# A prefetch hint on each engine for the branch over the general path, in an attention and gated feed-forward kernel

## The chip, the cores and the metric

The kernel runs on one core of a Trainium2 chip. The metric is the device time of one execution in microseconds; several runs are taken and their median is given. One further execution is recorded by the hardware profiler. Its trace names the engines PE (TensorE matmul), PEld (TensorE weight load), DVE (VectorE), ACT (ScalarE), POOL (GpSimd) and SP (SyncE); a trailing q (SPq, PEldq) marks an engine's instruction queue, in which branches, semaphore waits and DMA issues show.

## What is computed

For each of four batches, 32 inducing points attend to 12416 tokens of width 128, and the tokens attend to the result. A gated feed-forward layer with 1536 hidden units follows.

```python
h = mab(I, x)                      # softmax(I x^T * scale) x
y = mab(x, h)                      # softmax(x h^T * scale) h
gate = np.maximum(y @ w_gate, 0.0)
val = y @ w_val
out = (gate * val) @ w_out         # 49664 x 128
```

## The kernel before, in words

There are two ways through the program. `quadratic_kernel` computes the whole output by a form that holds as long as the sign of the gate of every hidden unit is the same for all tokens of a batch; four tests, one per batch, collect in `fine` for how many hidden units that is shown. At its end `left` is the number of units for which it is not (L1496 to L1511). `general_kernel` computes everything again in the ordinary way and runs only where `left` is above zero:

```python
left = quadratic_kernel(tc, *args)
with tc.If(left > 0):
    general_kernel(tc, *args)
```

The number is loaded into a register of each engine (L1512), each engine compares and branches (L1735), and with the inputs of this case all of them jump over the general path. The code of both ways lies one behind the other in each engine's program, and behind it the end of the program (L1762). On the short side of the branch each engine waits on one or more semaphores and goes on to the end; SP, which issues the stores, waits there for the eight DMA lanes of its transfers, one EVENT_SEMAPHORE for each.

In the way that runs, the tokens of a batch come in 12 blocks. For each block four pairs of score matmuls (L1341) are taken through an exponential on ACT (L1350), and the outputs of 128 tokens are summed by two runs of small matmuls (L1398); the second run stands behind a wait for the first (`after`). Three such outputs on each side make a unit. A unit is finished by a reciprocal `r{b}.{u}` (L1425) and a division `d{b}.{u}` (L1430) on VectorE, 16 units in a batch, and is then stored by SP (L1454; for the last two units of all, in four smaller stores, L1442).

Nothing reorders this work afterwards: the kernel schedules by hand. Each step is an `op` with its engine, its inputs and a function that emits its instructions. `plan.order` merges five fixed sequences, one for each engine, into one order by estimated starting times, and the loop at L1514 emits the steps in it:

```python
for o in plan.order(BEGIN, SEQUENCES, NEAR):
    if o.warm:
        keep_busy(*o.warm)
    if o.emit:
        o.emit()
```

`d3.13` (`B` is 4) is the third last division. In that order the last instructions ahead of it are, on ACT, the last exponential of the kernel; on VectorE the reciprocal `r3.13`; on SP the second store of unit 11's pair; on POOL the last step of the last test; on TensorE the end of one run of eight output matmuls, directly ahead of another run of eight.

Of the kernel before, what the change touches and what calls it, by code (L numbers as in the profile page):

```python
# [295 lines left out]
def quadratic_kernel(tc, x, inducing, moe_w_gate, moe_w_val, moe_w_out, out):  # L296
    with ExitStack() as ctx:
        return quadratic_body(
            ctx, tc, x, inducing, moe_w_gate, moe_w_val, moe_w_out, out
        )  # L300


def quadratic_body(ctx, tc, x, inducing, moe_w_gate, moe_w_val, moe_w_out, out):
    nc = tc.nc
    B, N, C = x.shape
# [85 lines left out]
    def main(shape, dtype, name):  # L391
        return mp.tile(shape, dtype, name=name)
# [83 lines left out]
    SYNC = mybir.DependencyInfo(mybir.DependencyClass.Sync, mybir.DependencyReason.DATA)  # L476
# [19 lines left out]
    def keep_busy(n, bank, part):  # L496

        for _ in range(4 * n if part else n):
            if part:
                pe.matmul(AL[:, bank, 400:BLK], ones16, ones16[:, 0 : BLK - 400], start=True, stop=True)  # L500
            else:
                pe.matmul(
                    AL[:, bank, :], ones16, ones16.unsqueeze(1).broadcast_to([P, 4, P]),
                    start=True, stop=True,
                )
# [989 lines left out]
    left = main([P, 1], mybir.dt.int32, "left")  # L1495
# [16 lines left out]
    op("load", "SP", 0.1, lambda: conds.append(nc.values_load(left[0:1, 0:1])), [(a, 1.5)])  # L1512
    quadratic_body.plan = plan
    for o in plan.order(BEGIN, SEQUENCES, NEAR):  # L1514
        if o.warm:
            keep_busy(*o.warm)
        if o.emit:
            o.emit()
# [205 lines left out]
def kernel(  # L1724
    tc: tile.TileContext,
    x: bass.AP,
    inducing: bass.AP,
    moe_w_gate: bass.AP,
    moe_w_val: bass.AP,
    moe_w_out: bass.AP,  # L1730
    out: bass.AP,
):
    args = (x, inducing, moe_w_gate, moe_w_val, moe_w_out, out)
    left = quadratic_kernel(tc, *args)
    with tc.If(left > 0):  # L1735
        general_kernel(tc, *args)


# [28 lines left out]
```

## Time and profile before

| | us |
|---|---|
| three runs, median | 270.16 |
| three runs, lowest and highest | 267.34 and 270.39 |
| the profiled execution | 268.36 |
| its span, first to last instruction | 266.5 |

TensorE is busy for 241.9 us of the span (91%), ACT for 222.7 (84%), VectorE for 180.0 (68%), GpSimd for 84.5 (32%). These shares count neither branches nor semaphore waits nor the issue of DMAs, so a stretch at the end in which only such instructions run shows as idle on every engine. The chain of waits, followed back from the last computation, gives TensorE 69% of the span, DMA 10%, ACT 9% and VectorE 4%. DMA moves 49.78 MB; two of its queues carry instructions and not data, and are listed as q8 and q14.

### The profile page before, as it was taken

What the parts mean: (1) busy time and instruction counts of PE and PEld (TensorE: products, weight loads), DVE (VectorE), ACT (ScalarE), POOL (GpSimd) and SP (SyncE); (2) the same over time, 40 slices, a digit from 0 to 9 for tenths busy, and PEclk for the clock granted to TensorE, in tenths of its full rate; (3) what the DMA queues carried; (4) which work ended last, traced back from release to release, by engine and by line L of the source; (5) the groups of instructions that cost most, each with busy time, mean ns of one, the idle gap of its engine ahead of it and who ended that gap; (6) DMA issues with size and microseconds to landing.
All of it is one profiled execution on the core that took longest, in us unless ns stands there. A gap on an engine that the chain in (4) does not pass through costs nothing.

```text
span 266.5 us, 12469 instructions
## 1 busy us (share of the span) xinstructions
PE 241.9 (91%) x5668; PEld 182.7 (69%) x5668; DVE 180.0 (68%) x377; ACT 222.7 (84%) x265; POOL 84.5 (32%) x145
## 2 busy tenths in 40 slices
PE   6889797889699999999999979999999999999970
PEld 2676565558476778777568867677777768878850
DVE  4457597785437898845779858755789895565550
ACT  3664798767669999999999968999999999999920
POOL 4476120399013000596130000197020008912000
PEclk9999999999869999999999999999999999999996
DMA  7999999959996986349999994033514333363552
GB/s 252 422 344 158 213 215 210 202 101 147 194 290 148 275 149 243 85 129 220 196 217 278 308 206 174 15 121 123 233 61 191 126 121 123 121 247 122 199 219 75
DMA packets 42653, 49.78 MB, mean 187 GB/s; under 512 B 29121, under 2 KB 30305, under 8 KB 42593
## 3 DMA queue, kind: packets, MB, share of 16 engines
q1 hardware_dynamic: 37680, 38.18, 47.5%
q0 software_dynamic: 4864, 10.72, 23.8%
q8 instruction: 46, 0.75, 1.2%
q14 instruction: 15, 0.11, 0.1%
q10 hardware_dynamic: 48, 0.02, 0.0%
HBM read 27.80 MB, written 25.43 MB: 200 GB/s over the span
## 4 chain that ended last, share of the span: by engine, by line
PE 69%; DMA 10%; ACT 9%; DVE 4%; issue 3%; SPq 2%; POOL 0%; ACTq 0%; DVEq 0%
PE AL L1398 35%; PE AL L1341 14%; ACT F L1350 7%; DMA F<-in_x_dram 6%; PE AL L1137 3%; DMA xTr<-x16r 3%; PE AL L925 2%; PE AL L957 2%; DMA out_dram<-osb 2%; PE AL L825 2%; PE AL L794 2%; DVE osb L1430 1%; PE AL L1156 1%; PE AL L500 1%; DVE u L1070 1%
## 5 line engine op out<-in xcount | busy, mean ns | idle before, releaser
L1350 ACT ACTIVATE F<-AL 128x1024 f16<-128x1024 f32 x192 | 184.4, 1037 | 15.7 <-PE AL L1341 12.8
L1398 PE MATMUL AL<-T,F 64*128 64x129 f16 x3456 | 136.3, 220 | 4.7 <-issue 3.3
L1398 PEld LDWEIGHTS <-F 64*128 64x128 f16 x3456 | 109.0, 95 | 34.4 <-PE AL L1398 20.5
L1341 PE MATMUL AL<-S,pairs 64*128 64x512 f16 x384 | 74.9, 382 | 1.4 <-ACT F L1350 0.6
L1430 DVE TENSOR_TENSOR osb<-AL,rzo 128x768 f32<-128x768 f32 x64 | 61.2, 957 | 3.2 <-DMA out_dram<-osb 1.2
L1201 POOL TENSOR_TENSOR far<-S 128x768 f16<-128x768 f16 x16 | 23.9, 1504 | 78.3 <-DVE U L1119 77.7
L1425 DVE RECIPROCAL rzo<-AL 128x6 f32<-128x6 f32 x64 | 12.6, 196 | 45.5 <-PE AL L1398 44.8
L1341 PEld LDWEIGHTS <-pairs 64*128 64x128 f16 x384 | 22.0, 94 | 8.9 <-issue 5.8
L1201 POOL TENSOR_TENSOR far<-far 128x768 f16<-128x768 f16 (+2 forms) x20 | 25.0, 1252 | 1.5
L375 POOL DMA_DIRECT2D x<-in_x_dram x18 | 9.8, 555 | 29.3 <-PE AL L825 22.3
L1119 DVE TENSOR_TENSOR U<-U 128x1536 f16<-128x1536 f16 x16 | 15.2, 949 | 0.2
L643 DVE COPY xT<-AL 128x1024 f16<-128x1024 f16 (+1 forms) x14 | 8.5, 615 | 8.9 <-PE AL L639 8.9
L1137 PE MATMUL AL<-wo,U 128*128 128x128 f16 x192 | 13.3, 220 | 0.7 <-issue 0.7
L624 ACT CAST x<-F 128x512 f16<-128x512 f32 (+1 forms) x14 | 7.7, 557 | 6.6 <-DMA F<-in_x_dram 6.6
L1137 PEld LDWEIGHTS <-U 128*128 128x128 f16 x192 | 10.8, 98 | 3.6 <-issue 2.6
L1241 POOL TENSOR_SCALAR eps<-eps 128x1 f32<-128x1 f32 x4 | 0.7, 187 | 32.7 <-DVE eps L1226 25.7
L754 DVE COPY xT<-AL 128x2048 f16<-128x2048 f16 x6 | 7.3, 1223 | 4.5 <-PE AL L744 4.3
L804 ACT ACTIVATE p<-AL 128x1024 f16<-128x1024 f32 x9 | 9.3, 1029 | 1.3 <-PE AL L794 1.3
L622 POOL CAST x<-F 128x512 f16<-128x512 f32 (+1 forms) x14 | 7.6, 554 | 8.2 <-DMA F<-in_x_dram 8.1
L639 PE MATMUL AL<-eye,x 128*128 128x128 f16 x96 | 7.9, 224 | 1.4 <-POOL x L622 1.3
L1090 DVE TENSOR_TENSOR U<-ga,va 128x768 f16<-128x768 f16 x16 | 8.8, 549 | 0.7 <-ACT va L485 0.6
L485 ACT ACTIVATE S<-AL 128x1024 f16<-128x1024 f32 x6 | 6.2, 1030 | 3.5 <-DVE hT L386 2.3
(157 smaller groups left out, 260.0 us busy)
## 6 DMA issues: line engine op xcount, KB each, us to landing
out_dram<-osb SPq DMA_DIRECT2D x62, 384.0 KB, 3.6
x<-in_x_dram POOLq DMA_DIRECT2D x18, 512.0 KB, 11.7
F<-in_x_dram SPq DMA_DIRECT2D x10, 512.0 KB, 7.2
F<-in_x_dram SPq DMA_DIRECT2D x4, 256.0 KB, 9.4
out_dram<-osb SPq DMA_DIRECT2D x4, 192.0 KB, 3.3
wg<-in_moe_w_gate_dram POOLq DMA_DIRECT2D x1, 384.0 KB, 5.9
wv<-in_moe_w_val_dram POOLq DMA_DIRECT2D x1, 384.0 KB, 5.8
wo<-in_moe_w_out_dram POOLq DMA_DIRECT2D x1, 384.0 KB, 7.5
```

Of the source, the lines that this page charges most:

```text
L375: pool.dma_start(out=x16(b, t0, n), in_=xv[b][:, t0 : t0 + n, :])
L643: dve.tensor_copy(out=xT(t0, n), in_=ps[:, 0:n, :])
L804: lambda o=o1, dst=dst: act.activation(out=dst.rearrange("p k t m -> p k (t m)"), in_=ebanks(o), func=AF.Exp, scale=sm_scale,),
L1090: s["product"] = dve.tensor_tensor(out=U[j % NU][:, i, :, odd:4:2, :], in0=a[:, :, 0:M].unsqueeze(2).broadcast_to([P, NFF, 2, M]), in1=win ...
L1119: s["product"] = dve.tensor_tensor(out=u0, in0=u0, in1=u1, op=ALU.add)
L1137: pe.matmul(dbank(first)[:, 0:P], U[j % NU][:, i, t].rearrange("p k m -> p (k m)"), wo[:, t, :], start=(i, t) == (0, 0), stop=(i, t) == (n ...
L1201: pool.tensor_tensor(out=dst, in0=in0, in1=in1, op=f)
L1341: pe.matmul(ebanks(o)[:, r, :], pairs[ROWS[r], par, j, :], S[b % 2][ROWS[r], g, :], start=True, stop=True,)
L1350: lambda o=o, j=j: act.activation(out=dst[:, j], in_=ebanks(o), func=AF.Exp, scale=sm_scale,),
L1398: pe.matmul(ps[:, k_, :], l, m_, start=step == 0 and j == 0, stop=step == 1 and j == n - 1,)
L1425: lambda: dve.reciprocal(out=rzo[rr], in_=view()[:, :, :, P : P + 1]),
L1430: lambda: dve.tensor_tensor(out=dst[:, :, 3 * h6 : 3 * h6 + 3, :], in0=view()[:, :, :, 0:P], in1=rzo[rr].broadcast_to([P, 2, 3, P]), op=AL ...
```

## The change

Ahead of the emission of `d3.13` one prefetch hint is put on each engine for the branch named `done`, with the side "likely taken". Each hint is made to depend on the last instruction that its engine has been given so far, by a semaphore dependency. The `If` gets the name `done`. Nothing else is changed.

```diff
     for o in plan.order(BEGIN, SEQUENCES, NEAR):
+        if o.name == f"d{B - 1}.13":
+
+            seen = nc.cur_bb.bb.instructions
+            n = len(seen)
+            tc.mark_branch_hint_location("done", hint="LikelyTaken", engines=tuple(mybir.ALL_ENGINES))
+            for y in nc.cur_bb.bb.instructions[n:]:
+                e = [z for z in seen[:n] if z.engine == y.engine][-1]
+                tc.add_manual_dep(y, e.name, SYNC, reason="behind what is issued")
         if o.warm:
             keep_busy(*o.warm)
         if o.emit:
@@
     left = quadratic_kernel(tc, *args)
-    with tc.If(left > 0):
+    with tc.If(left > 0, label="done"):
         general_kernel(tc, *args)
```

## The prediction

> **What bounds the kernel now.** I read the end of the program first, since the change touches only that. The chain of waits over its last stretch (start us, us, what):
>
> ```profile
> 254.21 0.66 PE AL L1398 x16
> 254.87 0.05 issue
> 254.92 1.77 PE AL L1398 x53
> ...
> 258.00 0.21 DVE rzo L1425
> ...
> 258.23 0.96 DVE osb L1430
> 259.19 0.07 DVE left L1505
> ```
>
> TensorE's output matmuls set the pace up to 258.0, then VectorE's last division, then `left`. The chain stops with it at 259.26 (259.19 + 0.07), but the span does not:
>
> ```profile
> span 266.5 us, 12469 instructions
> ```
>
> So 7.2 us stand behind the last computation. The rows of the branch and of what it jumps to (both L1735) show what fills them; the columns are engine queue, operation, count, duration in ns (min/median/max), first and last start in us:
>
> ```profile
> L1735 SPq EVENT_SEMAPHORE  x8: 17/17/17, 264.0 to 264.5; - x8
> L1735 ACTq COMPARE_BRANCH  x1: 50/50/50, 259.8 to 259.8; - x1
> L1735 POOLq COMPARE_BRANCH  x1: 45/45/45, 259.9 to 259.9; - x1
> L1735 PEldq COMPARE_BRANCH  x1: 3986/3986/3986, 259.9 to 259.9; - x1
> L1735 DVEq COMPARE_BRANCH  x1: 72/72/72, 259.9 to 259.9; - x1
> L1735 POOLq EVENT_SEMAPHORE  x1: 17/17/17, 260.0 to 260.0; - x1
> L1735 SPq COMPARE_BRANCH  x1: 53/53/53, 260.6 to 260.6; - x1
> L1735 ACTq EVENT_SEMAPHORE  x1: 17/17/17, 263.7 to 263.7; - x1
> L1735 PEldq EVENT_SEMAPHORE  x1: 51/51/51, 263.9 to 263.9; - x1
> ```
>
> Each engine branches once and then runs its next instruction, an EVENT_SEMAPHORE at the target. POOL needs 0.2 us for that (259.9 to 260.0, rounded up). ACT needs 3.9 us, PE 4.0 (here the record of the branch itself is 3986 ns long), SP 3.4 (260.6 to 264.0). POOL's general path is a handful of instructions, the others' hundreds to thousands. The DMA rows between 261.0 and 262.0 say what they wait for, instruction packets on queues 14 and 8:
>
> ```profile
> q14 instruction: 3, 0.02, 8.4%
> q8 instruction: 1, 0.02, 8.0%
> ```
>
> Whose they are shows the count in the whole span (the page's busy line and its DMA queue):
>
> ```profile
> PE 241.9 (91%) x5668; PEld 182.7 (69%) x5668; DVE 180.0 (68%) x377; ACT 222.7 (84%) x265; POOL 84.5 (32%) x145
> q8 instruction: 46, 0.75, 1.2%
> q14 instruction: 15, 0.11, 0.1%
> ```
>
> Queue 8 brought 46 packets of 16 KB (0.75 MB / 46) for 2 x 5668 PE records, one per 246: it is PE's. The three of queue 14, some 8 KB each, are one each for ACT, DVE and SP. So the jump costs SP a code fetch of about 3.2 us beyond POOL's 0.2. SP matters most: its eight waits at 264.0 to 264.5 and those behind it close the program.
>
> **The change part by part.** *What it can take away.* If the target is there, SP goes on at 260.6 + 0.2 = 260.8 instead of 264.0, and the others near 260.1. But SP's first job there is to wait for the stores to land, one DMA lane for each of its eight waits. The last stores (L1442), alone and as a pair:
>
> ```profile
> L1442 SPq DMA_DIRECT2D out_dram<-osb x1: 333/333/333, 259.2 to 259.2; - x1
> DMA to landing us min/median/max: 2.5/2.5/2.5
> L1442 SPq DMA_DIRECT2D out_dram<-osb x2: 333/378/423, 259.2 to 259.6; - x2
> DMA to landing us min/median/max: 2.5/3.1/3.7
> ```
>
> The store issued at 259.6 is thus the one of 3.7 us: it lands at 263.3. Of the 3.2 us only what is behind that landing can go. Now its landing is covered by the fetch; with the fetch gone it is the late one. From SP's wait to the end of the span stand 2.5 us if that lane is the first of the eight (264.0 to 266.5) and 2.0 if it is the last (264.5); I take the middle, 2.2. End: 263.3 + 2.2 = 265.5, a gain of 1.0 (0.7 to 1.2 by the lane).
>
> *What it adds: five hints, each behind the last instruction that its engine has been given.* The rows around 254 us (start us, us, engine, line, operation, idle before it):
>
> ```profile
> 252.82 1.97 ACT L1350 ACTIVATE F<-AL 128x1024 f16<-128x1024 f32 x2
> 253.90 0.20 DVE L1425 RECIPROCAL rzo<-AL 128x6 f32<-128x6 f32 x1 [0.57 <-PE AL L1398]
> 254.13 0.96 DVE L1430 TENSOR_TENSOR osb<-AL,rzo 128x768 f32<-128x768 f32 x1
> 254.21 0.47 PEld L1398 LDWEIGHTS <-F 64*128 64x128 f16 x16 [0.24 <-PE AL L1398]
> 254.91 1.57 PEld L1398 LDWEIGHTS <-F 64*128 64x128 f16 x54 [0.24 <-PE AL L1398]
> 255.11 0.81 SPq L1454 DMA_DIRECT2D out_dram<-osb  x2
> 256.24 0.20 DVE L1425 RECIPROCAL rzo<-AL 128x6 f32<-128x6 f32 x1 [1.16 <-PE AL L1398]
> ```
>
> d3.13 is the division at 254.13 (256.47 and 258.23 are the next two). No hint stands in this trace, so each is bounded by the nearest sequencer instructions, 17 to 72 ns in the branch rows.
> - POOL: it has run all its work but the load; nothing is queued behind. Cost nothing.
> - ACT: the last exponential (in the row at 252.82) ends at 254.8. Behind the hint stands only the load of `left`, which can't start before 259.26. Nothing; a fetch of 3.9 us begun at 254.8 is there at 258.7, ahead of ACT's branch at 259.8.
> - DVE: the hint waits for the reciprocal (ends 254.10), which d3.13 waits for too. d3.13 moves by one sequencer instruction, under 0.1 us. The cover is the 1.16 us that VectorE is idle ahead of the reciprocal at 256.24; SP's store at 255.11 moves by as much and isn't last. Without the cover it would be 0.1 on the path.
> - SP: its last instruction ahead of the hint is a store, so the hint waits for a landing. The two stores ahead:
>
> ```profile
> L1454 SPq DMA_DIRECT2D out_dram<-osb x2: 332/487/642, 251.2 to 251.5; - x2
> DMA to landing us min/median/max: 2.5/2.7/3.0
> ```
>
>   At the latest 251.5 + 3.0 = 254.5. Queued behind it is the store at 255.11, 0.6 us later: covered. Fetch there by 254.5 + 3.4 = 257.9, branch at 260.6.
> - PE: this one is on the path. In the order of the program the hint falls between two steps of eight matmuls that run as one row of 16 (254.21). It waits for the first eight to finish, so TensorE runs dry once more. Such a stop is the idle of 0.24 us ahead of the weight loads at 254.21 and 254.91; by the modelled ends of matmuls it is only the 0.05 of "issue" in the chain. I take 0.24, since the loads feed the array and the ends are modelled. Queued behind are the last outputs, for which the reciprocals r3.14 and r3.15, the last stores and `left` wait; no other wait in that chain is large enough to swallow it. The fetch: 254.5 + 4.0 = 258.5, branch at 259.9 + 0.24.
>
> *What it moves: instruction packets.* The four target packets leave 261 to 262 and come about 255 to 257, beside the stores there. That can cost or gain, since stores near a fetch land late. The stretches 251 to 254 (no instruction packet) and 254 to 257 (one):
>
> ```profile
> out_dram<-osb SPq DMA_DIRECT2D x2, 384.0 KB, 2.7
> q8 instruction: 1, 0.02, 3.6%
> out_dram<-osb SPq DMA_DIRECT2D x2, 384.0 KB, 4.5
> ```
>
> Same size, 2.7 against 4.5 us. So if the end is free of packets, the last store lands 2.5 us after its issue (its neighbour's row) and not 3.7: 1.2 better. Against it: after the jump the engines fetch the code behind the target (264 to 265, again three and one),
>
> ```profile
> q14 instruction: 3, 0.02, 8.4%
> q8 instruction: 1, 0.02, 7.0%
> ```
>
> and that would now come near 260.5 to 261.5, just where the target's packets come now. The worst row is 1.8 (4.5 less 2.7) later. I take no change, because the same four packets of the same size meet the same store; ends: 1.2 better, 1.8 worse.
>
> *Sum.* The last store is issued at 259.6 + 0.24 = 259.84, lands 3.7 later at 263.54; 2.2 to the end: 265.7 against 266.5, a gain of 0.8 us. Ends: 2.0 gained, 1.0 lost. The profiled execution took 268.36 us, 1.9 outside its span: 267.6. The three runs have a median of 270.16 (267.34 to 270.39), so on that scale 269.4.
>
> The Trainium skill ("Runtime: NRT & Kernel Launch", section "Instruction fetch mechanics") says that a taken branch to code outside the two blocks that an engine holds must fetch it first; this trace agrees, 3.4 to 4.0 us against POOL's 0.2. The same section calls prefetch purely sequential and counts two blocks of 16 KiB; the blocks of queue 14 are 8 KB here. With two places the target has to displace a block, which is the third rival; by that rule the sum would come out slower.
>
> **The rivals.**
> *The end runs free of packets.* The prefetcher takes the target in place of the block behind it, and what follows the jump comes too late to meet the store. For it: the neighbour at 2.5 us. Against: the packets at 264 to 265 come within 0.6 us of the jump's end. It gives 0.24 lost and 0.8 + 1.2 = 2.0 gained in all: 266.4 on the profiled scale, 268.2 on the median's.
>
> *The hint does nothing.* It is given too early or names the wrong side of the branch, or the block is lost again before the jump. All fetches stay, and PE's stop is paid: 268.6, or 270.4. For it: SP resumes only 0.7 us after the last landing, so even a half success shows little.
>
> *It pushes out code that is still needed.* Place: PE, right behind its hint. The single queue 8 packet between 254 and 257 is PE's regular fetch, which comes when PE enters a new block, so a boundary lies within some 2 us behind the hint and the block behind it has been fetched already. If the target takes that block's place, PE stands at the boundary for a fetch, 4.0 us (the branch's 3986 ns), and loses the target again: 0.24 + 4.0 = 4.2 slower, 272.6, or 274.4. It decides as soon as the boundary is reached before a second fetch is done, that is with under 4 us of matmuls left in the block. If the two fetches queue up it is up to 8 us. Against it: a prefetch that drops its own next block would help nobody.
>
> **How the numbers follow.** Forecast 0.53, free end 0.17, nothing 0.20, code pushed out 0.07, the rest 0.03. The time is the forecast's, 269.4. The runs of before differ by 3 us, more than all cases but the third rival, so the range is the lowest run less the gain, 267.34 - 0.8 = 266.5, to the highest with PE's stop, 270.39 + 0.24, rounded 270.7; that holds the first three cases and leaves out the third rival. Two per cent, 5.4 us, is about what a measurement of this kernel tells from no change. Faster by that needs nearly the whole 7.2 us behind `left`: 0.02. Slower by that needs the pushed out code with both fetches in a row: 0.03. Within: 0.95.
>
> **What would show it.** Right: SP's first EVENT_SEMAPHORE after its branch within 0.3 us, PE's branch record below 0.2 us, one of SP's eight waits held to about 263.5, four instruction packets about 255 to 257, one more weight load idle of about 0.24 near 254.5, a span of 265.7. Wrong: a branch record of 4 us on PE again (the hint does nothing), a gap of microseconds in PE's matmuls near 255 to 256 (code pushed out), landings of the last store at 2.5 us (free end), or a landing near 265, which would take the whole gain back.

## The result, and the profile after

| | before | after |
|---|---|---|
| median of 22 runs of each, taken side by side | 268.28 us (265.02 to 270.83) | 267.74 us (265.31 to 271.48) |
| ratio, with its 95% interval | | 0.9998 (0.997 to 1.0026) |
| profiled execution, its span | 266.5 us | 263.5 us |
| from the start of `left` (L1505) to the end of the span | 7.42 us | 7.49 us |

The ratio, here and below, leaves out executions that took over 1.5% longer than the fastest of the same kernel, so it isn't the quotient of the two medians. The change makes no difference that can be measured: 268.28 us x 0.003 is 0.8 us either way. The spans differ by 3 us, but that is there by 166 us (from the starts of the exponentials in both), long before the first hint at 239.6; both kernels' runs scatter by 6 us. What can be compared from one execution to the next is the stretch behind `left`, and it is what it was. The rows in which that stretch is read, the row of `left` in the timelines of before and of after, and the first line of the page of after:

```profile
259.11 0.15 DVE L1505 TENSOR_SCALAR left<-AL 128x1 int32<-128x1 f32 x1
```
```profile
256.03 0.15 DVE L1505 TENSOR_SCALAR left<-AL 128x1 int32<-128x1 f32 x1
```
```profile
span 263.5 us, 12474 instructions
```

The branch and what it jumps to (queue, operation, count, ns, first and last start in us), now L1743:

```profile
L1743 SPq EVENT_SEMAPHORE  x8: 17/17/17, 261.3 to 261.8; - x8
L1743 ACTq COMPARE_BRANCH  x1: 68/68/68, 256.8 to 256.8; - x1
L1743 POOLq COMPARE_BRANCH  x1: 65/65/65, 256.8 to 256.8; - x1
L1743 DVEq COMPARE_BRANCH  x1: 84/84/84, 256.8 to 256.8; - x1
L1743 PEldq COMPARE_BRANCH  x1: 483/483/483, 256.8 to 256.8; - x1
L1743 POOLq EVENT_SEMAPHORE  x1: 17/17/17, 257.3 to 257.3; - x1
L1743 PEldq EVENT_SEMAPHORE  x1: 51/51/51, 257.4 to 257.4; - x1
L1743 SPq COMPARE_BRANCH  x1: 73/73/73, 257.6 to 257.6; - x1
L1743 ACTq EVENT_SEMAPHORE  x1: 17/17/17, 261.0 to 261.0; - x1
L1743 DVEq EVENT_SEMAPHORE  x1: 21/21/21, 261.0 to 261.0; - x1
```

PE's branch record fell from 3986 to 483 ns, and PE goes on 0.5 us after it: on PE the hint works. ACT and DVE still stand for 4.2 us (256.8 to 261.0) and SP for 3.7 (257.6 to 261.3). SP goes on last, and its waits close the program. Before, ACT and DVE stood for 3.8 us and SP for 3.35; the row of DVE's return in that profile is

```profile
L1735 DVEq EVENT_SEMAPHORE  x1: 21/21/21, 263.7 to 263.7; - x1
```

The hints themselves, and the instruction packets between 257.5 and 259 us:

```profile
L1770 POOLq BRANCH_PREFETCH_HINT  x1: 46/46/46, 239.6 to 239.6; - x1
L1770 SPq BRANCH_PREFETCH_HINT  x1: 55/55/55, 249.0 to 249.0; - x1
L1770 ACTq BRANCH_PREFETCH_HINT  x1: 50/50/50, 250.6 to 250.6; - x1
L1770 DVEq BRANCH_PREFETCH_HINT  x1: 56/56/56, 250.8 to 250.8; - x1
L1770 PEldq BRANCH_PREFETCH_HINT  x1: 50/50/50, 251.2 to 251.2; - x1
```
```profile
q14 instruction: 4, 0.03, 7.2%
q8 instruction: 1, 0.02, 6.0%
```

All five ran, 5.7 us or more ahead of the branch, at 46 to 56 ns each. But the fetches of ACT, DVE and SP still come at the jump, one packet of queue 14 more than before. Between 250 and 257.5 us queue 14 brought nothing; the only instruction packet there is one of queue 8, PE's. So on three engines the hint started no fetch at all.

PE did not stop either. Its hint stands at 251.2, in the middle of these rows of the timeline of after, which are those of before at 254.21 and 254.91:

```profile
251.13 0.47 PEld L1398 LDWEIGHTS <-F 64*128 64x128 f16 x16 [0.24 <-PE AL L1398]
251.84 1.57 PEld L1398 LDWEIGHTS <-F 64*128 64x128 f16 x54 [0.24 <-PE AL L1398]
```

The 16 loads run through, 0.47 us as before. The dependency on the same engine's last instruction only fixes the place; the hint waits for nothing, on SP either (249.0 us, no landing awaited).

### The profile page after: what moved, and what is told of

Same layout as the page of the kernel before. It is cut to its first block, busy times and chain, and to the rows that moved or that the text cites. A ratio compares the mean times of both kernels' runs of the same rounds, so it can differ in the third digit from the quotient of the medians.

```text
span 263.5 us, 12474 instructions
## 1 busy us (share of the span) xinstructions
PE 239.2 (91%) x5668; PEld 181.0 (69%) x5668; DVE 179.6 (68%) x377; ACT 222.9 (85%) x265; POOL 84.9 (32%) x145
## 4 chain that ended last, share of the span: by engine, by line
PE 66%; DMA 12%; ACT 9%; DVE 4%; issue 3%; SPq 2%; POOL 0%; DVEq 0%; ACTq 0%
PE AL L1398 34%; PE AL L1341 14%; ACT F L1350 7%; DMA F<-in_x_dram 5%; DMA out_dram<-osb 4%; PE AL L1137 3%; DMA xTr<-x16r 3%; PE AL L925 2%; DVE osb L1430 2%; PE AL L825 2%; PE AL L794 2%; PE AL L957 1%; SPq L762 1%; PE AL L1156 1%; PE AL L500 1%
## 5 line engine op out<-in xcount | busy, mean ns | idle before, releaser
L1398 PE MATMUL AL<-T,F 64*128 64x129 f16 x3456 | 134.1, 217 | 4.7 <-issue 3.1
L1398 PEld LDWEIGHTS <-F 64*128 64x128 f16 x3456 | 106.9, 94 | 33.8 <-PE AL L1398 20.2
L1341 PE MATMUL AL<-S,pairs 64*128 64x512 f16 x384 | 73.9, 377 | 1.2 <-ACT F L1350 0.6
L794 PEld LDWEIGHTS <-xT 128*128 128x128 f16 x288 | 8.0, 96 | 1.6 <-issue 0.7
(157 smaller groups left out, 261.0 us busy)
```

What stands on the lines that cost most here:

```text
L794: pe.matmul(ps[:, i, t, :], xTs[q][:, t, :], indT, start=True, stop=True)
L1341: pe.matmul(ebanks(o)[:, r, :], pairs[ROWS[r], par, j, :], S[b % 2][ROWS[r], g, :], start=True, stop=True,)
L1398: pe.matmul(ps[:, k_, :], l, m_, start=step == 0 and j == 0, stop=step == 1 and j == n - 1,)
```

## The experiments

One theory explains PE's success and the others' failure: a hint starts nothing by itself; it only changes which block is fetched when the engine enters the block of code that holds the branch. PE's stood ahead of that entry, the others behind it. The rivals: the hint can act on PE only; it acts on the next fetch only, and so must stand close; it needs more time than the 6 to 9 us that it had.

The experiments move the hints, or give them to some engines only, with the kernel otherwise as after the change. In each POOL has no hint unless it is named. Where no ratio is given there is one execution only, the profiled one, and its total time is not compared. The lines that differ:

```diff
-        if o.name == f"d{B - 1}.13":
+        if o.name in HINTS:
-            tc.mark_branch_hint_location("done", hint="LikelyTaken", engines=tuple(mybir.ALL_ENGINES))
+            tc.mark_branch_hint_location("done", hint="LikelyTaken", engines=tuple(getattr(mybir.EngineType, e) for e in HINTS[o.name]))
```

"Stretch" below is always from the start of the instruction that writes `left` to the end of the span, and "resumes" the time from an engine's branch to its next instruction.

**One block ahead** (e_block).

```diff
+HINTS = {'d0.12': ['SP'], 'd2.4': ['DVE'], 'd2.8': ['Activation'], 'd3.13': ['PE']}
```

> Each hint is moved one block of code ahead of its branch: on SP, DVE and ACT to places from which the engine still has to enter the block that holds the branch; PE's stays, POOL's is left out. Measured by the stretch from the start of the tensor_scalar that writes `left` to the end of the span, 7.4 us before (259.11 to 266.52) and 7.5 us after the change. Theory 1 (a hint acts only when the engine enters the branch's block, by choosing what is fetched next; after that it does nothing): ACT, DVE and SP run their next instruction within 0.6 us of their branch, as PE did, three 8 KB packets go from the end to earlier places, the last landing plus 2.2 us ends the program, and the stretch is 5.4 to 6.5 us. Theory 2 (only PE's hint can act, whatever its place): 7.5 us, branches of ACT, DVE and SP 3.4 to 4.3 us as now.

Measured: SP resumes after 0.53 us, ACT 0.48, DVE 0.60, PE 0.55; stretch 4.65 us. Over 13 runs the ratio to before is 0.9917 (0.9873 to 0.9961): under two per cent, but clear of 1. The hint is not PE's alone. The stretch is even shorter than theory 1 gave, since the last store landed 2.2 us after its issue, and not 3.7, and from the landing to the end it was 1.9 us and not 2.2.

**Far ahead** (e_far).

```diff
+HINTS = {'d0.4': ['SP', 'DVE', 'Activation', 'PE']}
```

> The hints of SP, DVE, ACT and PE are put ahead of the first batch's fifth division, some 34 blocks ahead of the branch on PE and two on DVE and ACT. If a hint is held until the engine enters the branch's block: as e_block, PE's branch to its next instruction 0.5 us, stretch from `left` to the end 5.4 to 6.5 us. If a hint acts on the next fetch only (and is lost, or pushes out code): PE misses again, 4 us at the branch, stretch about 7.5 us, and gaps of 3 to 4 us in PE, DVE and ACT at the first block boundary behind the hint.

Measured: the hints run at 74 to 77 us, 180 us ahead; the same 0.48 to 0.60 us on all four, stretch 5.17 us. A hint is held over all the blocks that lie between it and the branch, some 34 of them on PE.

**At the top** (e_top), with `HINTS` as in e_far and the dependency left out, which lets the hints rise to the top of each engine's program.

> The dependency of the hints is left out, so that they stand as each engine's fourth instruction (SP, DVE, ACT, PE). If a hint is held however far ahead: as e_far and e_block, a stretch of 5.4 to 6.5 us. If it is lost over that distance: 7.5 us with misses of 3.4 to 4.3 us on all four.

Measured: hints at 0.7 to 0.8 us, the same hits, stretch 4.99 us. Timed in a second run (e_top5):

> The kernel of e_top again, timed: hints at the top of SP, DVE, ACT and PE, none on POOL. The stretch behind `left` was 4.99 us against 7.42 before, so 2.4 us of 268, a ratio of 0.991; if what is gained at the end is lost to code fetches elsewhere, 0.997 to 1.003.

Measured: 0.9901 (0.9866 to 0.9936) over 12 runs, stretch 4.92 us. So 268.4 us, the median of before beside it, become about 265.8 (the median of this version's own 12 runs is 266.1). Like e_block it is faster than before, by about 1%. The kernel with the change was not run beside these two; its own ratio to before was 0.9998. The branch rows of this profile (L1739) and its last store:

```profile
L1739 SPq EVENT_SEMAPHORE  x8: 17/17/17, 260.4 to 261.5; - x8
L1739 ACTq COMPARE_BRANCH  x1: 68/68/68, 259.0 to 259.0; - x1
L1739 PEldq COMPARE_BRANCH  x1: 482/482/482, 259.1 to 259.1; - x1
L1739 DVEq COMPARE_BRANCH  x1: 84/84/84, 259.1 to 259.1; - x1
L1739 ACTq EVENT_SEMAPHORE  x1: 17/17/17, 259.5 to 259.5; - x1
L1739 PEldq EVENT_SEMAPHORE  x1: 51/51/51, 259.7 to 259.7; - x1
L1739 DVEq EVENT_SEMAPHORE  x1: 21/21/21, 259.7 to 259.7; - x1
L1739 SPq COMPARE_BRANCH  x1: 73/73/73, 259.9 to 259.9; - x1
```
```profile
L1444 SPq DMA_DIRECT2D out_dram<-osb x2: 333/378/424, 258.4 to 258.8; - x2
DMA to landing us min/median/max: 2.4/2.4/2.5
```

All four engines go on after 0.6 us or less. SP's eight waits now take 1.1 us from first to last (260.4 to 261.5) where they took 0.5 before: they stand for the store issued at 258.8, which lands 2.5 us later, at 261.3. The landing is the late one now, as the prediction had it. In all of e_block, e_far, e_top and e_top5 the stretch is the same sum: 0.5 us to the issue of the last store, 2.2 to 2.7 to its landing, and 1.9 from there to the end.

**At the edge** (e_edge). The three kernels above can't tell "ahead of the block" from "early enough". This one sets each hint close to the entry.

```diff
+HINTS = {'d1.12': ['SP'], 'd2.10': ['DVE'], 'd3.6': ['Activation'], 'd3.14': ['PE']}
```

> Each hint close to the place where its engine enters the block of the branch, as the fetches of before date it: SP, DVE and PE a few instructions behind that place (SP about 100 us and DVE about 55 us ahead of the branch, PE about 4 us), ACT a few instructions ahead of it (about 20 us). Theory 1 (the choice is made on entering the block): ACT alone goes on within 0.6 us of its branch; SP, DVE and PE miss, 3.4 to 4.3 us, and the stretch from `left` to the end is 7.4 to 7.6 us. Rival (the hints of the change were only too short before the branch, 6 to 9 us, for the fetch to be taken up): SP, DVE and ACT hit, PE misses, stretch 6.0 to 6.5 us.

The hints, and queue 14's packets in three stretches, 144 to 145 us (SP's and ACT's), 192 to 193 (DVE's) and 245 to 246 (ACT's, its last):

```profile
L1771 SPq BRANCH_PREFETCH_HINT  x1: 55/55/55, 156.2 to 156.2; - x1
L1771 DVEq BRANCH_PREFETCH_HINT  x1: 51/51/51, 204.6 to 204.6; - x1
L1771 ACTq BRANCH_PREFETCH_HINT  x1: 50/50/50, 238.2 to 238.2; - x1
L1771 PEldq BRANCH_PREFETCH_HINT  x1: 50/50/50, 255.4 to 255.4; - x1
```
```profile
q14 instruction: 2, 0.02, 5.1%
q14 instruction: 1, 0.01, 1.9%
q14 instruction: 1, 0.01, 2.3%
```

Whose packet is whose was read from where each engine stood in its program at the time. By that SP's and DVE's packets came some 12 us before their hint, and ACT's 7 us after. PE's packet is the only one of queue 8 between 255 and 256 us, at 255.7:

```profile
q8 instruction: 1, 0.02, 6.0%
```

That is 0.4 us behind PE's hint (255.4), but the fetch was begun ahead of it: at the jump PE's packet comes 1.4 us after the branch that asks for it (259.1 and 260.5). By the same lag, an estimate, this one was asked for at about 254.4. In the change, where PE's hint works, the packet comes 1.9 us behind the hint (251.2 and 253.0). The branch rows:

```profile
L1744 SPq EVENT_SEMAPHORE  x8: 17/17/17, 263.6 to 264.2; - x8
L1744 ACTq COMPARE_BRANCH  x1: 68/68/68, 259.0 to 259.0; - x1
L1744 PEldq COMPARE_BRANCH  x1: 3991/3991/3991, 259.1 to 259.1; - x1
L1744 DVEq COMPARE_BRANCH  x1: 84/84/84, 259.1 to 259.1; - x1
L1744 ACTq EVENT_SEMAPHORE  x1: 17/17/17, 259.5 to 259.5; - x1
L1744 SPq COMPARE_BRANCH  x1: 73/73/73, 259.9 to 259.9; - x1
L1744 DVEq EVENT_SEMAPHORE  x1: 21/21/21, 263.4 to 263.4; - x1
```

ACT alone goes on at once, with a hint 21 us ahead. SP misses with a hint 104 us ahead, DVE with one 55 us ahead, and PE, which worked in its old place, with one 4 us ahead. PE's miss is a whole one, 3991 ns, not the rest of a fetch that was begun late. So the lead in time doesn't decide; on which side of the entry the hint stands does. The runs bracket the entry without the reading of the packets too: a hint at 190 us works for DVE (e_block) and one at 205 doesn't, for ACT one at 238 works and one at 251 (the change) doesn't, for SP one at 109 works (e_block) and one at 156 doesn't. Stretch 7.53 us.

**SP alone** (e_sp).

```diff
+HINTS = {'d0.12': ['SP']}
```

> The hint on SP alone, at its early place. Theory 1 with the landing as the bound: SP's waits are what ends the program and ACT, DVE and PE have till about 4 us after their branch, so nearly all of the gain is there: SP resumes within 0.6 us, PE, ACT and DVE miss, the stretch from `left` to the end is 6.2 to 6.5 us. If the other engines' fetches bind as much: 7.2 to 7.5 us. If a hint on SP can't act: 7.5 us.

Measured: SP resumes after 0.53 us, the others miss, stretch 6.53 us. That is just above the theory's range, and it is made up otherwise: SP's waits stand from 263.6 to 266.4 for a store that took 4.1 us to land.

```profile
L1744 SPq EVENT_SEMAPHORE  x8: 17/17/17, 263.6 to 266.4; - x8
```
```profile
L1444 SPq DMA_DIRECT2D out_dram<-osb x1: 424/424/424, 262.1 to 262.1; - x1
DMA to landing us min/median/max: 4.1/4.1/4.1
```

262.1 + 4.1 is 266.2, and PE, ACT and DVE were back at 266.4 to 266.6, so either could have held the end. SP's waits behind the eight show which did: none is longer than 28 ns, so SP found every other engine back when it asked.

```profile
L1771 SPq EVENT_SEMAPHORE  x14: 17/28/28, 266.5 to 268.0; - x14
```

The landing held it, and the sum is that of the other kernels: 0.5 + 4.1 + 1.9 = 6.5. The next kernel shows what PE costs where the store lands early.

**SP, DVE and ACT, not PE** (e_late).

```diff
+HINTS = {'d0.12': ['SP'], 'd2.4': ['DVE'], 'd2.8': ['Activation']}
```

> The hints of SP, DVE and ACT at the working places, PE without one. PE's branch takes 4.0 us and its semaphore comes 4.8 us after `left` starts, as before; SP asks for it in the eleventh of its last twelve waits, from which 1.3 us remain to the end (265.20 to 266.52 before). So the stretch is 6.1 to 6.3 us if the stores have landed by then: about 1.2 less than before, and about 1.2 more than with PE's hint. If PE doesn't matter: 4.6 to 5.2 us.

Measured: 5.90 us, 0.2 below the forecast. PE resumes after 4.04 us, and SP's waits behind the jump (L1771) hold one of 1324 ns where all were 17 or 28:

```profile
L1771 SPq EVENT_SEMAPHORE  x14: 17/28/1324, 259.9 to 262.7; - x14
```

The stores had landed at 259.6. Landing and 1.9 us would end the program at 261.5; it ended at 262.8, 1.3 us later. So with the landing early PE's miss holds the end, and PE needs its hint as well as SP. Whether ACT's or DVE's miss alone would cost anything, no run tests.

**The last store on ACT's queue** (e_act5), on top of the far hints.

```diff
-    lambda k_=k_: nc.sync.dma_start(
+    lambda k_=k_, h6=h6: (act if h6 and k_ else nc.sync).dma_start(
```

> e_far, with the very last store issued by ACT and not behind its neighbour on SP. If the landing of the last store is what ends the program now (landing plus 1.9 us), the issue comes 0.4 us earlier and the stretch behind `left` is 4.3 to 4.8 us instead of 4.6 to 5.2; if the issue order doesn't matter, because one slow part of the last stores lands late anyway, it stays at 4.6 to 5.2 us.

Measured: both last stores start at 257.86, they land 2.4 and 2.8 us later, stretch 4.90 us; ratio 0.9892 (0.9845 to 0.9939) over 6 runs. The stretch lies among the 4.65 to 5.17 us of the versions without this edit: the pair issued at once has landed 2.9 us after `left`, where one after the other it had after 2.7 to 3.2. Beyond the hints this edit gives nothing that these runs can show.

**One hint of the change at a time**, PE's (e_pe) and then POOL's (e_pool).

```diff
+HINTS = {'d3.13': ['PE']}
```
```diff
+HINTS = {'d3.13': ['Pool']}
```

> Only PE's hint of the change, in its place; the others are left out. If the four other hints did nothing: PE goes on 0.5 us after its branch, SP, ACT and DVE miss as with the change, and the stretch from `left` to the end is 7.4 to 7.5 us. If the useless hints cost something at the end (SP resumed 0.4 us later behind its branch than before, 3.73 against 3.35, and POOL 0.3 later), SP and POOL are back at 3.35 and 0.18, and the stretch is about 7.1 us.

> Only POOL's hint of the change, in its place. If that hint costs POOL the 0.3 us at its branch and brings the fourth packet of queue 14 at the jump: 0.5 us at POOL, four packets, stretch 7.5 us or a little more. If these come from something else that all the kernels with hints share (such as where the code is laid), the same without any doing of the hint; e_pe, without POOL's hint, then shows 0.5 us and four packets too.

Measured: with PE's alone the stretch is 7.49 us, with POOL's alone 7.45. SP resumes after 3.73 and 3.70 us, POOL after 0.48 and 0.50, and queue 14 brings four packets at the jump in both. So PE's working hint is worth nothing by itself, POOL's useless one costs nothing by itself, and the 0.4 us by which SP is later behind its branch than before belongs to neither. It comes in every kernel with a hint in which SP misses (3.70 to 3.77 us), and ACT and DVE, where they miss, are later by as much (4.2 to 4.3 against 3.8), while PE's 4.0 stays. The fourth packet, on the queue that these three share, may be what delays them; why it comes, no run here tells.

## Why the prediction was right or wrong

*The time*, 267.74 us, lay in the range, and "no change that can be told" held. That was the width of the range, and not the mechanism: 266.5 to 270.7 us holds the forecast, the free end and the rival in which nothing happens, and the gain that was forecast, 0.8 us, did not come about.

*What bounds the end* was right: SP goes on last, its jump is a code fetch, and behind the fetch stands the last landing. The experiments that remove the fetch show it in that order.

*"If the target is there"* is the step that failed. The prediction let the fetch begin at the hint ("a fetch of 3.9 us begun at 254.8 is there at 258.7", and so for SP by 257.9). No fetch begins at a hint. The hint only changes the one that is made when the engine enters the branch's block, and ACT, DVE and SP had entered theirs long before. They still stood 4.2, 4.2 and 3.7 us at the jump, and of the forecast 0.8 us nothing came. The prediction used PE's block boundary, read from the single packet of queue 8, only for the third rival and never asked the same of the other engines; the packets of queue 14 give it. Where a hint does work, SP goes on after 0.53 us, and not the 0.2 taken from POOL; the wait for the landing hides the difference.

*The rival "the hint does nothing"* is what happened on the three engines that count, but for a reason that it didn't name: too late, where it said too early. Too early is what the runs exclude, up to 259 us ahead. Its 0.24 us for PE's stop did not occur.

*PE's stop of 0.24 us* was wrong: the hint carries no wait, and the matmuls run through. *SP's wait for a landing* was wrong for the same reason; the covers of ACT, DVE and POOL were not needed.

*Pushed out code* did not happen. PE's hint took the place of the block behind the branch, which is never run, and the page counts 45 packets of queue 8 where before had 46.

*The landing* was mis-sized: 3.7 us in before, 3.0 in the change (where the fetch still hid it) and 2.2 to 2.7 in the four profiles e_block, e_far, e_top and e_top5, in which all four hints work. So was what follows it: the prediction took 2.2 us, the middle of two lanes, and measured are 1.9. With a landing of 2.5 the rival of a free end forecast a gain of 2.0 us; those four gained 2.2 to 2.8 in the stretch. But its reason, an end free of packets, is not what they show: in e_top5 four packets of queue 14 come 1.5 to 2.1 us after the issue of the last store, as the three of before did (1.6 to 2.0), and it lands in 2.5 us. In e_edge, with three misses, it lands in 2.5 us too, in e_sp, e_pe and e_pool in 4.1. What makes a landing late is left open.

*Why the time stood still although PE was 3.5 us sooner:* SP asks PE for its semaphore near the end of its own waits, and those began 5.25 us after `left`, against 4.88 before; from there to the end it was 2.23 us against 2.54. The two differences nearly cancel, and neither is PE's.

The Trainium skill ("Runtime: NRT & Kernel Launch", section "Instruction fetch mechanics") calls prefetch purely sequential. Without a hint the traces agree (before, a packet for the code behind a branch that is always taken); with one they don't: PE's next packet is the target's, and the branch costs 0.5 us instead of 4.0. The measurement decides.

## What to carry to other kernels

Idle time behind the last computation is a place to look: here the code fetches at a branch over code that never runs took 2.2 to 2.8 us of the stretch behind `left`, and the chain of waits did not show it. A prefetch hint has to stand ahead of the block in which the branch lies, on each engine for whose branch the end waits (SP and PE here); in these runs the earliest place worked as well as any, for 45 to 60 ns on the engine's queue. When several engines meet at the end, ask each of them for the evidence that you found for one: the prediction dated the entry into the block on PE alone.

## What the runs showed of the hardware

- A hint is held from the first microsecond to the branch: with hints at 0.7 to 0.8 us the jump at 259 to 261 us took 0.5 to 0.6 us (e_top, e_top5).
- Given after the engine has entered the branch's block, it does nothing, even with 104 us to go (SP in e_edge).
- A jump over this code took 0.46 to 0.60 us where the target had been fetched by a hint and 3.35 to 4.3 us where it had not; a hint instruction takes 45 to 60 ns, and PE's matmuls ran on behind it (0.47 us for 16 weight loads, with and without).
- Code comes in packets of 16 KB on PE (queue 8) and 8 KB on the others (queue 14).
